# Attention scores from q and k as loaded: float32 matmuls on two row halves of the array in place of float32r parts

## Chip, core and metric

One core of a Trainium2 chip. The metric is the device time of one execution in microseconds (us); lower is better. A Trainium2 core has five engines with queues of their own: TensorE (PE in the rows, with its weight loads as PEld), VectorE (DVE), ScalarE (ACT), GpSimd (POOL) and SyncE (SP), which issues most of the DMAs.

## What is computed

Attention with a threshold, then a sum of four experts, then a squared-ReLU network. All inputs are float32, but for the last network's weights, which come as float64 and are narrowed on the chip during the experts. Batch 2, 8 heads, 576 positions, head size 64; 1152 tokens of 512 features.

```python
scores = q @ k.T / sqrt(64)                       # per head, 576 x 576
thresh = max(scores, axis=-1) - tau
p = exp(where(scores >= thresh, scores, -1e9) - max)
x = (p / (sum(p, axis=-1) + 1e-9)) @ v            # heads side by side: 1152 x 512
y = sum over e of pn[:, e] * (relu(x @ w1[e]) @ w2[e])   # 4 experts, 1024 wide
out = relu(y @ w_in) ** 2 @ w_out                 # 2048 wide
```

## The kernel before, in words

**Two stages.** Attention works through eight *units* u; a unit is a pair of heads z = 0, 1 of one batch entry. Behind it comes a dense stream: `first` and `second` for four experts and for the two halves of the last network, with weights split into a high and a low float32r part.

**A unit.** The 576 queries of a head are four tiles of 128 and a rest of 64; the rests of both heads share a ninth tile, the corner (k = 8). `qk` (L333) makes a score tile of 128 queries by 576 keys in PSUM, as two halves g of 288 keys. `rowmax` (L348) takes the negated maximum on VectorE; `threshold` (L352) makes one number per query from it and tau, as a difference of two 128x1 tensors; `expo` (L365) is the exponential on ScalarE; `mask` (L369) on VectorE compares the scores with the threshold, multiplies, and sums the row; `addeps` and `recip` give the row's reciprocal; `norm` (L385) multiplies p with it on GpSimd, and `norm_corner` (L393) does so for 64 more columns of the corner on VectorE. `turn` transposes p on TensorE (L402), `evac` copies the result to SBUF, mostly on ScalarE, and `pv` (L451) multiplies with v: float32 matmuls of 288 columns, the two heads on two halves of the array's columns. A mask frees the PSUM tile of its scores; there are three such tiles.

**q and k.** float32r matmuls take operands that are rounded, so `qk` works on parts. For units 1 to 7, `load_qk` (L263) loads 128 rows of 640 columns each of q and k, `q_scale` (L316) multiplies q by 1/8 on ScalarE, `high` (L307) rounds on ScalarE, `low` (L311) subtracts on GpSimd, and `stack` (L320) copies the parts between partitions by twelve DMAs a unit of 160 KB, so that a tile holds the high part of q over its low part, and two tiles hold the high and the low part of k twice. Two matmuls per half, one with each k tile, then give all four products; a score tile is four matmuls, the corner's eight. For unit 0, `start_qk` (L281) loads q and k of each head by a broadcast DMA that writes both halves of the partitions,

```python
nc.sync.dma_start(r[:, y], src[0][y * D:(y + 1) * D].unsqueeze(0).to_broadcast([2, D, r.shape[-1]]))   # L288
```

and makes the parts in place on three engines.

**Order.** The order on every engine is written out: each step of unit u is an event at the time u plus a number from the tables `WHEN` and `OWN`, and the events are sorted (L531). So TensorE meets scores, transposes and PV runs of neighbouring units in turn, and a step waits, in its place, for what it needs; what is behind it on its engine waits too.

Of the kernel before, what the change touches and what calls it, by code (L numbers as in the profile page):

```python
# [17 lines left out]
B, H, S, D = 2, 8, 576, 64  # L18
# [3 lines left out]
P = 128  # L22
NP = H // 2
NU = B * NP
QT = S // P
SQ = (QT + 1) * P
REM = S - QT * P
KC = 2 * QT + 1
# [31 lines left out]
    "q_scale": -2.100,  # L60
    "q_high": -1.890,
    "q_low": -1.695,
    "k_high": -1.456,
    "k_low": -1.025,
    "stack": (-0.339, -0.512, -1.282, -0.686),
    "load_v": 0.670,
# [45 lines left out]
        "q_scale": -12.152,  # L112
        "q_high": -9.978,
        "q_low": -9.096,
        "k_high": -12.288,
        "k_low": -10.414,
        "stack": (-9.241, -9.711, -7.013, -4.366),
    },
    2: {
        "load": -14.310,  # L120
        "q_scale": -7.271,
        "q_high": -4.013,
        "q_low": -1.805,
        "k_high": -10.466,
        "k_low": -6.537,
        "stack": (-1.315, -3.462, -1.279, -0.580),
    },
# [30 lines left out]
def attention_moe_kernel(ctx, tc, qT, kT, vp, tau, probs, wa, wb, wc, wd, out):  # L158
    nc = tc.nc
# [14 lines left out]
    qsc = const.tile([P, 1], F32, name="qsc")  # L174
    tneg = const.tile([P, 1], F32, name="tneg")
# [74 lines left out]
    pt_p = tail.enter_context(tc.tile_pool(name="pt", bufs=2))  # L250
# [22 lines left out]

    def new_qk(u):
        qs[u] = qk_p.tile([P, 2, SQ], F32R, tag="q1", name=f"q1{u}")
        ks[u] = (
            qk_p.tile([P, 2, SQ], F32R, tag="k1", name=f"k1{u}"),
            qk_p.tile([P, 2, SQ], F32R, tag="k2", name=f"k2{u}"),
        )

    def start_qk():  # L281
        new_qk(0)
        stage = pt_p.tile([P, KC, S], F32, tag="pt", name="stage").rearrange("p c s -> p (c s)")
        rq = stage[:, :2 * SQ].rearrange("p (y n) -> p y n", y=2)
        rk = stage[:, 2 * SQ:4 * SQ].rearrange("p (y n) -> p y n", y=2)
        for y in range(2):
            for r, src in ((rk, kT), (rq, qT)):
                nc.sync.dma_start(r[:, y], src[0][y * D:(y + 1) * D].unsqueeze(0).to_broadcast([2, D, r.shape[-1]]))  # L288
        q1, (k1, k2) = qs[0], ks[0]
        nc.vector.tensor_scalar(rq[:, 0], rq[:, 0], qsc, None, ALU.mult)  # L290
        nc.gpsimd.tensor_mul(rq[:, 1, P:], rq[:, 1, P:], qsc.to_broadcast([P, SQ - P]))
        nc.scalar.copy(k1[:, 0], rk[:, 0])
        nc.vector.tensor_sub(k2[:, 0], rk[:, 0], k1[:, 0].bitcast(F32))
        nc.scalar.copy(q1[:, 0, :P], rq[:, 0, :P])
        nc.vector.tensor_sub(q1[D:P, 0, :P], rq[D:P, 0, :P], q1[D:P, 0, :P].bitcast(F32))
        nc.scalar.copy(k1[:, 1], rk[:, 1])
        nc.vector.tensor_sub(k2[:, 1], rk[:, 1], k1[:, 1].bitcast(F32))
        nc.scalar.activation(q1[:, 1, :P], rq[:, 1, :P], AF.Copy, scale=qsc)
        nc.vector.scalar_tensor_tensor(  # L299
            q1[D:P, 1, :P], rq[D:P, 1, :P], qsc[D:P], q1[D:P, 1, :P].bitcast(F32), ALU.mult, ALU.subtract  # L300
        )
        nc.scalar.copy(q1[:, 0, P:], rq[:, 0, P:])
        nc.gpsimd.tensor_sub(q1[D:P, 0, P:], rq[D:P, 0, P:], q1[D:P, 0, P:].bitcast(F32))
        nc.scalar.copy(q1[:, 1, P:], rq[:, 1, P:])
        nc.gpsimd.tensor_sub(q1[D:P, 1, P:], rq[D:P, 1, P:], q1[D:P, 1, P:].bitcast(F32))

    def high(u, n):  # L307
        parts.setdefault(u, {})[n] = t = raw_p.tile([P, SQ], F32R, tag=f"high{n}", name=f"high{n}_{u}")
        nc.scalar.copy(t, raws[u][n])

    def low(u, n):  # L311
        raw, t = raws[u][n], parts[u][n].bitcast(F32)
        parts[u][2 + n] = o = raw_p.tile([P, SQ], F32R, tag=f"low{n}", name=f"low{n}_{u}")
        nc.gpsimd.tensor_sub(o, raw, t)

    def q_scale(u):  # L316
        rq = raws[u][0]
        nc.scalar.activation(rq, rq, AF.Copy, scale=qsc)

    def stack(u, n):  # L320
        if u not in qs:
            new_qk(u)
        for y in range(2):
            src = parts[u][n][y * D:(y + 1) * D].bitcast(F32)
            for z in ((n // 2,), (0, 1))[n % 2]:
                o = (qs[u], ks[u][n // 2])[n % 2]
                nc.sync.dma_start(o[z * D:(z + 1) * D, y].bitcast(F32), src)

    HW = S // 2
    W = 2 * QT + 1  # L330
    s_t, p_t, nm_t, th_t, sm_t, r_t, pt_t, t_t, pv_t, xs_t = ({} for _ in range(10))

    def qk(u, k):  # L333
        i, z = divmod(k, 2)
        s = ps_s.tile([P, 2, 512], F32, tag="s", name=f"s{u}_{k}")
        for g in range(2):
            a = g * HW
            if i < QT:
                ops = [(qs[u][:, z, i * P:(i + 1) * P], k[:, z, a:a + HW]) for k in ks[u]]
            else:  # L340
                ops = [
                    (qs[u][:, y, QT * P:], k[:, y, a + y * REM:a + y * REM + HW]) for y in range(2) for k in ks[u]
                ]
            for x, (w, k) in enumerate(ops):
                nc.tensor.matmul(s[:, g, :HW], w, k, start=(x == 0), stop=(x == len(ops) - 1))  # L345
        s_t[u, 2 * i + z] = s[:, :, :HW]

# [61 lines left out]
    idle = [0]  # L409
# [65 lines left out]
    def at(u, t, f, *args):  # L475
        events.append((u + t, len(events), f, (u,) + args))

    for u in range(NU):
        when = {**WHEN, **OWN.get(u, {})}
# [14 lines left out]
        if u:  # L494
            at(u, when["load"], load_qk)
            at(u, when["q_scale"], q_scale)
            for n, t in enumerate(when["stack"]):
                at(u, t, stack, n)
            for n, x in enumerate("qk"):
                at(u, when[x + "_high"], high, n)  # L500
                at(u, when[x + "_low"], low, n)

# [259 lines left out]
```

## Time and profile before

| | |
|---|---|
| median of 3 runs | 802.04 us (801.55 to 802.53) |
| the profiled execution | 802.34 us |
| its span, first to last instruction | 800.0 us |
| mean granted TensorE clock | 0.978 |
| busy in the span | PE 755.7, DVE 367.5, ACT 292.3, POOL 275.5 us |
| bytes moved by DMA | 75.66 MB |

The profile is of one execution. A group of rows gives a view of it: *slices* cut the span in 40 equal parts, each digit the busy tenths of one; *stretches* give the busy time of each engine between two times; a *timeline* lists instructions by their start, with repeats of one form taken together, and in brackets how long the engine had been idle and what released it; *groups* take together all instructions of a line and form. A DMA row gives the time that its issue took on the queue. Starts and durations of matmuls overlap, since they are pipelined, so the step from one start to the next says more than a duration. PV appears as two records per float32 matmul. Times count from the span's start.

### The profile page before, as it was taken

Reading aid. Unit: us, or ns where it says so; the run is one execution under the profiler, and the core shown is the slowest. Engines: PE = TensorE matmul, PEld = TensorE weight load, DVE = VectorE, ACT = ScalarE, POOL = GpSimd, SP = SyncE. Lnnn points to the kernel's source line nnn. Section 1 sums busy time; section 2 is a strip of 40 time slices with the busy share of each in tenths; the row PEclk is TensorE's granted clock in tenths of the full one; section 3 lists DMA queues with packets and bytes.
Section 4 is the critical chain, followed back from the end, with each engine's and each line's share of the span. In section 5 each row is a group of like instructions: output and inputs, shape, how many; then the busy total and the mean of one; then the engine's idle time right before and its main releaser. Section 6 shows DMA issues by size and latency. Waiting matters only on the chain.

```text
span 800.0 us, 10387 instructions
## 1 busy us (share of the span) xinstructions
PE 755.7 (94%) x4052; PEld 657.1 (82%) x4052; DVE 367.5 (46%) x723; ACT 292.3 (37%) x524; POOL 275.5 (34%) x201
## 2 busy tenths in 40 slices
PE   3289999999999999999999999999999999999998
PEld 2266666657898889988899888998889988899886
DVE  0499999993644336643354333664422210022111
ACT  1378888763342013321133201331225531255200
POOL 0387777761323112220222211221126641266300
PEclk7589999999999999999999999999999999999999
DMA  1477685300534314441344332333101110010011
GB/s 42 121 204 211 150 229 131 99 18 1 197 132 153 110 67 131 133 132 39 132 132 125 94 110 74 125 132 106 39 27 53 53 54 26 27 53 1 17 50 53
DMA packets 28056, 75.66 MB, mean 95 GB/s; under 512 B 3816, under 2 KB 3816, under 8 KB 28008
## 3 DMA queue, kind: packets, MB, share of 16 engines
q1 hardware_dynamic: 27976, 75.01, 30.4%
q8 instruction: 32, 0.52, 0.3%
q14 instruction: 16, 0.13, 0.1%
q0 software_dynamic: 32, 0.00, 0.0%
HBM read 50.48 MB, written 10.75 MB: 77 GB/s over the span
## 4 chain that ended last, share of the span: by engine, by line
PE 77%; DVE 12%; DMA 4%; issue 3%; ACT 2%; SPq 1%; ACTq 0%; POOL 0%; DVEq 0%; POOLq 0%
PE po L633 37%; PE ph L556 36%; DVE p L374 5%; DMA stage<-in_qT_dram 3%; DVE th L354 3%; DVE nm L350 2%; PE pv L451 2%; PE s L345 1%; SPq L288 1%; DMA wraw<-in_wa_dram 1%; PE t L402 1%; DVE pm L374 1%; ACT p L367 1%; DVE sm L379 1%; PE x2t L650 0%
## 5 line engine op out<-in xcount | busy, mean ns | idle before, releaser
L212 POOL TENSOR_TENSOR wlo<-wraw,whi 128x1024 fp32r<-128x1024 f32 x48 | 115.5, 2405 | 375.0 <-ACT whi L210 323.3
L556 PE MATMUL ph<-xhi,whi 128*128 128x384 f32 x576 | 196.1, 340 | 1.9 <-DVE hlo L600 1.8
L556 PE MATMUL ph<-xlo,whi 128*128 128x384 f32 x576 | 194.8, 338 | 0.0
L556 PE MATMUL ph<-xhi,wlo 128*128 128x384 f32 x576 | 194.8, 338 | 0.0
L633 PE MATMUL po<-whi,hhi 128*128 128x512 f32 x432 | 168.8, 391 | 0.0
L633 PE MATMUL po<-whi,hlo 128*128 128x512 f32 x432 | 168.2, 389 | 0.0
L633 PE MATMUL po<-wlo,hhi 128*128 128x512 f32 x432 | 168.1, 389 | 0.0
L556 PEld LDWEIGHTS ph<-xhi,whi 128*128 128x128 f32 x576 | 108.1, 188 | 4.3 <-issue 2.8
L556 PEld LDWEIGHTS ph<-xlo,whi 128*128 128x128 f32 x576 | 108.1, 188 | 0.2
L556 PEld LDWEIGHTS ph<-xhi,wlo 128*128 128x128 f32 x576 | 108.1, 188 | 0.0
L345 PE MATMUL s<-k,q 128*128 128x288 f32 x320 | 64.7, 332 | 34.2 <-DVE q L299 12.4
L633 PEld LDWEIGHTS po<-whi,hlo 128*128 128x128 f32 x432 | 81.1, 188 | 17.1
L633 PEld LDWEIGHTS po<-wlo,hhi 128*128 128x128 f32 x432 | 81.1, 188 | 16.4
L633 PEld LDWEIGHTS po<-whi,hhi 128*128 128x128 f32 x432 | 81.1, 188 | 16.3
L345 PEld LDWEIGHTS s<-k,q 128*128 128x128 f32 x320 | 48.2, 202 | 44.6 <-DVE q L299 12.8
L604 DVE SCALAR_TENSOR_TENSOR u<-ph,u 128x384 f32<-128x384 f32 x48 | 26.8, 558 | 123.5 <-ACT u L603 123.5
L600 DVE SCALAR_TENSOR_TENSOR hlo<-ph,hhi 128x384 fp32r<-128x384 f32 x96 | 53.0, 554 | 61.6 <-ACT hhi L599 61.5
L238 ACT ACTIVATE wide<-wide 128x512 f32<-128x512 f32 x32 | 21.4, 669 | 162.6 <-DVE dbl L237 159.4
L391 POOL TENSOR_TENSOR p<-p,r 128x576 f32<-128x576 f32 x60 | 68.0, 1148 | 31.6 <-DVE th L354 9.8
L599 ACT ACTIVATE hhi<-ph 128x384 fp32r<-128x384 f32 x96 | 45.7, 489 | 84.4 <-PE ph L556 84.4
L611 POOL TENSOR_TENSOR hlo<-u,hhi 128x384 fp32r<-128x384 f32 x48 | 48.5, 1016 | 32.7 <-ACT hhi L610 32.7
L640 DVE SCALAR_TENSOR_TENSOR acc<-po,pn,acc 128x512 f32<-128x512 f32 x27 | 20.3, 751 | 83.8 <-PE po L633 83.8
(83 smaller groups left out, 773.7 us busy)
## 6 DMA issues: line engine op xcount, KB each, us to landing
wraw<-in_wa_dram SPq DMA_DIRECT2D x16, 512.0 KB, 4.1
wide<-in_wc_dram SPq DMA_DIRECT2D x16, 512.0 KB, 3.7
wraw<-in_wb_dram SPq DMA_DIRECT2D x16, 512.0 KB, 4.3
narrow<-dbl SPq DMA_DIRECT2D x32, 256.0 KB, 2.4
wide<-in_wd_dram SPq DMA_DIRECT2D x16, 512.0 KB, 3.6
wraw<-narrow SPq DMA_DIRECT2D x16, 512.0 KB, 3.2
k<-high SPq DMA_DIRECT2D x28, 160.0 KB, 3.0
k<-low SPq DMA_DIRECT2D x28, 160.0 KB, 5.0
```

The costliest lines, as they stand in the source:

```text
L212: engine.tensor_sub(lo, t, hi.bitcast(F32))
L238: nc.scalar.activation(m, m, AF.Square)
L345: nc.tensor.matmul(s[:, g, :HW], w, k, start=(x == 0), stop=(x == len(ops) - 1))
L354: nc.vector.tensor_sub(th_t[u, k], tneg, nm_t[u, k])
L374: nc.vector.scalar_tensor_tensor(p, s_t.pop((u, k)), th_t[u, k], p, ALU.is_ge, ALU.mult, accum_out=sm_t[u, i][:, z:z + 1])
L391: nc.gpsimd.tensor_mul(p, p, r_t[u, i][:, z:z + 1].to_broadcast([P, S]))
L556: nc.tensor.matmul(o, w, m, start=a, stop=b)
L599: nc.scalar.activation(oh, p, AF.Relu)
L600: nc.vector.scalar_tensor_tensor(ol, p, 0.0, oh.bitcast(F32), ALU.max, ALU.subtract)
L604: nc.vector.scalar_tensor_tensor(r, p, 0.0, r, ALU.max, ALU.mult)
L611: nc.gpsimd.tensor_sub(ol, r, oh.bitcast(F32))
L633: nc.tensor.matmul(o, w, m, start=(x == 0), stop=(x == len(ops) - 1))
```

## The change

The scores become true float32 matmuls on q and k as they were loaded. The host lays q out as 64 rows for both heads, and repeats it in the other 64 partitions; k is laid out so that partitions 0 to 63 hold its first 288 keys and partitions 64 to 127 the other 288 (head 0, head 1 with its rest first, and head 1 in plain order, which the corner uses). Half g of a score tile is then one matmul over rows 64g to 64g + 63 of the array, and a tile is two matmuls, which write separate parts of the score tile; the corner's are four, each on 64 rows and 64 columns. The parts, their copies, `start_qk`'s work on three engines and their events go. A unit loads 576 KB of q and 432 KB of k, into four buffers instead of two; unit 0 loads them head by head. Two more edits: `threshold` becomes a scalar operation (nm times -1, plus tneg read as one number per partition), and `norm_corner` moves to GpSimd, except at the end, where the kernel puts normalisation on VectorE. The other entries of the tables stay.

```diff
     def load_qk(u):
-        rq = raw_p.tile([P, SQ], F32, tag="rq", name=f"rq{u}")
-        rk = raw_p.tile([P, SQ], F32, tag="rk", name=f"rk{u}")
-        nc.sync.dma_start(rq, qT[u])
-        nc.sync.dma_start(rk, kT[u])
+        qs[u] = qk_p.tile([P, 2, S], F32, tag="q", name=f"q{u}")
+        ks[u] = qk_p.tile([P, 3, HW], F32, tag="k", name=f"k{u}")
+        if u:
+            nc.sync.dma_start(qs[u], qT[u])
+            nc.sync.dma_start(ks[u], kT[u])
+        else:
+            for z in range(2):
+                nc.sync.dma_start(qs[u][:, z], qT[u][:, z])
+                nc.sync.dma_start(ks[u][:, z:z * 2 + 1], kT[u][:, z:z * 2 + 1])
...
+    def q_scale(u):
+        nc.scalar.activation(qs[u], qs[u], AF.Copy, scale=qsc)
...
     def start_qk():
-        new_qk(0)
...
+        load_qk(0)
+        for z in range(2):
+            nc.vector.tensor_scalar(qs[0][:, z], qs[0][:, z], qsc, None, ALU.mult)
...
     def qk(u, k):
...
+        cols = slice(i * P, min(i * P + P, S))
+        for y in (z,) if i < QT else range(2):
+            o = s if i < QT else s[y * REM:(y + 1) * REM]
+            for g in range(2):
+                rows = slice(g * D, (g + 1) * D)
+                nc.tensor.matmul(
+                    o[:, g, :HW], qs[u][rows, y, cols], ks[u][rows, y if i < QT else 2 * y], start=True, stop=True
+                )
...
     def threshold(u, k):
-        nc.vector.tensor_sub(th_t[u, k], tneg, nm_t[u, k])
+        nc.vector.tensor_scalar(th_t[u, k], nm_t[u, k], -1.0, tneg, ALU.mult, ALU.add)
...
     def norm_corner(u):
-        nc.vector.tensor_scalar(p[:, S:], p[:, QT * P:S], r_t[u, QT], None, ALU.mult)
+        if idle[0]:
+            nc.vector.tensor_scalar(p[:, S:], p[:, QT * P:S], r_t[u, QT], None, ALU.mult)
+        else:
+            nc.gpsimd.tensor_mul(p[:, S:], p[:, QT * P:S], r_t[u, QT].to_broadcast([P, REM]))
```

Removed with no successor: `new_qk`, `high`, `low`, `stack`, the pool `raw`, and the table entries `q_high`, `q_low`, `k_high`, `k_low` and `stack`.

What the engines then meet, in order, at three places (the numbers in a name count tiles as they are made, and differ between the kernels). **SP's queue from the start**, before, with the copies of unit 1 at its end:

```order
L288 DMA stage<-in_kT_dram 128x1x640
L288 DMA stage<-in_qT_dram 128x1x640
L288 DMA stage<-in_kT_dram 128x1x640
L288 DMA stage<-in_qT_dram 128x1x640
L530 DMA pr<-in_probs_dram 128x36
L266 DMA rq_171<-in_qT_dram 128x640
L267 DMA rk_172<-in_kT_dram 128x640
L266 DMA rq_198<-in_qT_dram 128x640
L267 DMA rk_199<-in_kT_dram 128x640
L327 DMA k_236<-high_1_215 64x640 x4
```

and after the change:

```order
L257 DMA q_115<-in_qT_dram 128x576
L258 DMA k_116<-in_kT_dram 128x288
L257 DMA q_115<-in_qT_dram 128x576
L258 DMA k_116<-in_kT_dram 128x576
L468 DMA pr<-in_probs_dram 128x36
L253 DMA q_152<-in_qT_dram 128x1152
L254 DMA k_153<-in_kT_dram 128x864
L253 DMA q_175<-in_qT_dram 128x1152
L254 DMA k_176<-in_kT_dram 128x864
```

The four broadcasts have become four plain loads, and nothing is copied between partitions behind the loads. **TensorE late in a steady unit** (t a transpose run, s a score run, pv a PV run), before:

```order
L402 MATMUL t_0_1052<-ident,p_0_886 128x128 x4
L345 MATMUL s_7_1057<-k_600,q_599 128x288
L345 MATMUL s_7_1057<-k_601,q_599 128x288
L345 MATMUL s_7_1057<-k_600,q_599 128x288
L345 MATMUL s_7_1057<-k_601,q_599 128x288
L451 MATMUL pv_0_1043<-pt_801,rv_815 64x288 x2
L402 MATMUL t_7_1074<-ident,p_3_808 128x128 x4
```

and after the change, with the corner behind it:

```order
L345 MATMUL t_0_1094<-ident,p_0_953 128x128 x4
L283 MATMUL s_7_1099<-k_564,q_563 128x288 x2
L394 MATMUL pv_0_1087<-pt_877,rv_890 64x288 x2
L345 MATMUL t_7_1114<-ident,p_3_1108 128x128 x4
L283 MATMUL s_8_1123<-k_564,q_563 64x288 x4
```

The runs stand in the same turn; a score run has two matmuls instead of four, the corner's four instead of eight. **VectorE around a corner**, before:

```order
L379 TENSOR_SCALAR sm_3_1095<-sm_3_1095 128x2
L354 TENSOR_TENSOR th_0_1161<-tneg,nm_0_1138 128x1
L379 TENSOR_SCALAR sm_4_1153<-sm_4_1153 128x1
L383 RECIPROCAL r_3_1172<-sm_3_1095 128x2
L354 TENSOR_TENSOR th_1_1174<-tneg,nm_1_1155 128x1
L383 RECIPROCAL r_4_1177<-sm_4_1153 128x1
L395 TENSOR_SCALAR pm_1126<-pm_1126,r_4_1177 128x64
```

and after the change:

```order
L319 TENSOR_SCALAR sm_3_900<-sm_3_900 128x2
L294 TENSOR_SCALAR th_0_957<-nm_0_936,tneg 128x1
L319 TENSOR_SCALAR sm_4_949<-sm_4_949 128x1
L323 RECIPROCAL r_3_966<-sm_3_900 128x2
L294 TENSOR_SCALAR th_1_968<-nm_1_951,tneg 128x1
L323 RECIPROCAL r_4_971<-sm_4_949 128x1
L314 SCALAR_TENSOR_TENSOR p_0_953,sm_0_984<-s_0_907,th_0_957,p_0_953 128x576
```

The thresholds are another operation in the same place, and the corner's product is gone from this engine; the next mask follows at once.

## Rows read from the trace of the kernel before

**Rows 1.** The page's slices of the span: TensorE's busy tenths, 20 us a slice.

```profile
PE   3289999999999999999999999999999999999998
```

**Rows 2.** Stretches: length, engines' busy us (instructions), granted clock, DMA share, GB/s.

```profile
0.00:20.00 20.00, 6.50 (x28) 5.96 (x28) 1.89 (x5) 2.51 (x4) 1.41 (x7) 0.77 0.11 42
20.00:31.25 11.25, 0.21 (x1) 0.00 (x0) 0.83 (x1) 0.72 (x1) 0.00 (x0) 0.50 0.49 149
...
122.27:140.95 18.68, 17.48 (x123) 12.06 (x121) 18.58 (x49) 15.02 (x30) 14.67 (x14) 1.00 0.49 125
```

**Rows 3.** Timeline of VectorE at the start: start, duration, instruction [idle before, releaser].

```profile
7.51 0.15 DVE L523 TENSOR_SCALAR qsc<-tau_t 128x1 f32<-128x1 f32 x1 [7.51 <-DMA tau_t<-in_tau_dram]
...
17.22 0.55 DVE L290 TENSOR_SCALAR stage<-stage,qsc 128x640 f32<-128x640 f32 x1 [9.33 <-DMA stage<-in_qT_dram]
...
32.59 0.76 DVE L350 TENSOR_REDUCE nm<-s 128x1 f32<-128x576 f32 x1
```

**Rows 4.** Timeline of SP's queue, its first load: start and time to issue.

```profile
0.75 0.70 SPq L288 DMA_DIRECT2D stage<-in_kT_dram  x1
```

**Rows 5.** Timelines of GpSimd and VectorE around 116 us.

```profile
115.29 2.25 POOL L391 TENSOR_TENSOR p<-p,r 128x576 f32<-128x576 f32 x2 [1.18 <-DVE r L383]
...
116.42 1.13 DVE L354 TENSOR_TENSOR th<-tneg,nm 128x1 f32<-128x1 f32 x1
```

**Rows 6.** Groups of VectorE, four units: line, form, count, busy, mean ns, idle before.

```profile
L354 DVE TENSOR_TENSOR th<-tneg,nm 128x1 f32<-128x1 f32 x36 | 18.3, 509 | 0.1
L395 DVE TENSOR_SCALAR pm<-pm,r 128x64 f32<-128x64 f32 x4 | 4.5, 1117 | 0.1
...
L379 DVE TENSOR_SCALAR sm<-sm 128x2 f32<-128x2 f32 x16 | 2.9, 181 | 0.0
...
L379 DVE TENSOR_SCALAR sm<-sm 128x1 f32<-128x1 f32 x4 | 0.6, 140 | 0.0
```

**Rows 7.** Waits of TensorE, four units: us in total, times, longest.

```profile
PE s L345 <- DVE p L374: 3.7, 7, 1.0
```

**Rows 8.** Timelines of VectorE (first and last unit) and TensorE (last unit).

```profile
36.86 0.96 DVE L354 TENSOR_TENSOR th<-tneg,nm 128x1 f32<-128x1 f32 x1
...
168.63 2.41 DVE L354 TENSOR_TENSOR th<-tneg,nm 128x1 f32<-128x1 f32 x2
...
172.03 0.79 PE L345 MATMUL s<-k,q 128*128 128x288 f32 x4 [1.48 <-DVE p L374]
```

**Rows 9.** DMA issues of the span: count, KB each, median us to landing.

```profile
rv<-in_vp_dram SPq DMA_DIRECT2D x8, 320.0 KB, 5.3
...
rq<-in_qT_dram SPq DMA_DIRECT2D x7, 320.0 KB, 12.1
```

**Rows 10.** Groups of the whole span, ScalarE's scaling of q.

```profile
L318 ACT ACTIVATE rq<-rq,qsc 128x640 f32<-128x640 f32 x7 | 5.9, 836 | 0.0
```

**Rows 11.** Timeline of TensorE in steady units: start, first start to last end.

```profile
115.56 0.77 PE L345 MATMUL s<-k,q 128*128 128x288 f32 x4
116.26 0.71 PE L451 MATMUL pv<-pt,rv 128*64 128x288 f32 x4
116.90 0.66 PE L402 MATMUL t<-ident,p 128*128 128x128 f32 x4
117.31 1.31 PE L345 MATMUL s<-k,q 128*128 128x288 f32 x8
118.46 0.60 PE L402 MATMUL t<-ident,p 128*128 128x128 f32 x4
...
121.50 1.19 PE L451 MATMUL pv<-pt,rv 128*64 128x288 f32 x8
122.62 0.66 PE L402 MATMUL t<-ident,p 128*128 128x128 f32 x4
...
129.75 0.78 PE L345 MATMUL s<-k,q 128*128 128x288 f32 x4
130.36 0.60 PE L429 MATMUL tr<-ident,p 128*128 128x128 f32 x4
```

More of the change, by code (lines that the diff above doesn't have):

```diff
@@ L60 @@
     "q_scale": -2.100,
[L61 to L65, printed above, removed]
     "load_v": 0.670,
@@ L112 @@
         "q_scale": -12.152,
[L113 to L117, printed above, removed]
     },
@@ L121 @@
         "q_scale": -7.271,
[L122 to L126, printed above, removed]
     },
@@ L254, in attention_moe_kernel @@
     head = ExitStack()
-    raw_p = head.enter_context(tc.tile_pool(name="raw", bufs=2))
-    qk_p = head.enter_context(tc.tile_pool(name="qk", bufs=2))
+    qk_p = head.enter_context(tc.tile_pool(name="qk", bufs=4))
     p_p = head.enter_context(tc.tile_pool(name="p", bufs=6))
@@ L259, in attention_moe_kernel @@
     ps_s = head.enter_context(tc.tile_pool(name="ps_s", bufs=3, space=PSUM))
-    raws, parts, qs, ks, vs = {}, {}, {}, {}, {}
+    qs, ks, vs = {}, {}, {}
+    HW = S // 2
     def load_qk(u):
-        rq = raw_p.tile([P, SQ], F32, tag="rq", name=f"rq{u}")
-        rk = raw_p.tile([P, SQ], F32, tag="rk", name=f"rk{u}")
-        nc.sync.dma_start(rq, qT[u])
-        nc.sync.dma_start(rk, kT[u])
-        raws[u] = (rq, rk)
+        qs[u] = qk_p.tile([P, 2, S], F32, tag="q", name=f"q{u}")
[7 more added lines that the diff above has]
+                nc.sync.dma_start(ks[u][:, z:z * 2 + 1], kT[u][:, z:z * 2 + 1])
     def load_v(u):
@@ L272, in load_v @@
         nc.sync.dma_start(vs[u], vp[u])
[L274 to L279, printed above, removed]
-    def start_qk():
-        new_qk(0)
[L283 to L327, printed above, removed]
@@ L329, in attention_moe_kernel @@
-    HW = S // 2
+    def q_scale(u):
+        nc.scalar.activation(qs[u], qs[u], AF.Copy, scale=qsc)
+    def start_qk():
+        load_qk(0)
+        for z in range(2):
+            nc.vector.tensor_scalar(qs[0][:, z], qs[0][:, z], qsc, None, ALU.mult)
     W = 2 * QT + 1
@@ L335, in qk @@
         s = ps_s.tile([P, 2, 512], F32, tag="s", name=f"s{u}_{k}")
[L336 to L345, printed above, removed]
+        cols = slice(i * P, min(i * P + P, S))
[6 more added lines that the diff above has]
+                )
         s_t[u, 2 * i + z] = s[:, :, :HW]
@@ L496, in attention_moe_kernel @@
             at(u, when["q_scale"], q_scale)
[L497 to L501, printed above, removed]
     def load_weights(u):
@@ L719, in pairs_t @@
         return a.reshape(NU, 2, S, D).transpose(0, 1, 3, 2)
-    qp = _np.zeros((NU, 2, D, SQ), q.dtype)
-    qp[..., :m] = pairs_t(q)[..., :m]
-    for z in range(2):
-        qp[:, z, :, m + z * REM:m + (z + 1) * REM] = pairs_t(q)[:, z, :, m:]
-    kt = pairs_t(k).copy()
-    kt[:, 1] = _np.concatenate([kt[:, 1, :, m:], kt[:, 1, :, :m]], axis=-1)
+    qp = pairs_t(q).transpose(0, 2, 1, 3)
+    kt = pairs_t(k)
+    rolled = _np.concatenate([kt[:, 1, :, m:], kt[:, 1, :, :m]], axis=-1)
+    kt = _np.stack([kt[:, 0], rolled, kt[:, 1]], axis=2).reshape(NU, D, 3, 2, S // 2).transpose(0, 3, 1, 2, 4)
     vh = v.reshape(NU, 2, S, D)
@@ L738 @@
     given = {
-        "qT": qp.reshape(NU, P, SQ),
-        "kT": _np.concatenate([kt, kt[..., :REM]], axis=-1).reshape(NU, P, SQ),
+        "qT": _np.concatenate([qp, qp], axis=1),
+        "kT": kt.reshape(NU, P, 3, S // 2),
         "vp": vp,
```

## The prediction

> **What bounds the kernel now.** I read the slices of the span first. From 200 us on TensorE's tenths stand at 9 in every slice but the last [rows 1]: the experts are one dense stream of matmuls, whose weights are loaded and split by events placed relative to it. A microsecond saved before them is a microsecond saved at the end, and nothing in the change touches them. So the attention stage is the whole question, and it has three stretches.
>
> *The start.* Over the first 20 us the DMA share is 0.11 at 42 GB/s and the granted clock averages 0.77 [rows 2]. VectorE has its scale factor at 7.51 us but gets q only at 17.22, and the first row maximum starts at 32.59 [rows 3]. Four broadcast loads stand at the head of SP's queue, the first issued at 0.75 [rows 4].
>
> *The steady units* (one pair of heads each). In the unit from 122.27 to 140.95 VectorE is busy for 18.58 of 18.68 us, TensorE for 17.48 [rows 2]. VectorE is not working all that time: a threshold of one element per partition starts at 116.42 and lasts 1.13 us, ending when GpSimd's pair of normalisations, started at 115.29 for 2.25 us, ends [rows 5]. Over four units thresholds average 509 ns, and the 64-column corner normalisation 1117 ns, while a 128x1 scalar operation takes 140 ns [rows 6]. So the bound reads VectorE, held by GpSimd, with TensorE about 1 us behind. What TensorE waits for in four units is 3.7 us behind the mask [rows 7], 0.92 us a unit, out of 18.68 - 17.48 = 1.2 us idle.
>
> *The end of attention.* Two thresholds take 2.41 us at 168.63, and TensorE idles 1.48 us before its next scores, behind the mask [rows 8].
>
> **The change, part by part.** *The start.* The broadcasts, their high and low parts and the copies go; four plain loads of 128 partitions and two scalings on VectorE stay. Plain loads of 320 KB land 5.3 us after issue (v) or 12.1 us after it (q, in the median; the first of them stood behind the broadcasts) [rows 9]. Issued 0.7 us apart from 0.75 on [rows 4], the third load, q of the second head, which VectorE scales before it takes any maximum, lands at 2.15 + 5.3 = 7.5 us, or at 14.3 by the far end. I take the first, since the broadcasts ahead are gone. tau arrives at 7.51 [rows 3]. Then qsc and tneg (0.4 us), two scalings (0.55 us for 640 columns [rows 3], so at most 1.1 us) and what is left of the first score's own time behind the second scaling (I allow 0.3 us): the first maximum starts at about 9.3 us in place of 32.59, so **-23.3 us**; -24.2 if tau, no longer behind broadcasts, comes before that load (7.5 + 0.55 + 0.3 = 8.4), and -17.3 by the late end. The second unit's loads now follow at once; its scaling on ScalarE has two exponentials ahead of it.
>
> *Thresholds and corner on VectorE.* The threshold becomes a scalar operation with one tensor input. Nearest is the 128x1 addition of epsilon: 140 ns, against 181 for the 128x2 form [rows 6]. Per unit this removes 9 x (0.509 - 0.140) = 3.3 us, and the corner's move removes 1.1, so VectorE needs 18.58 - 4.4 = 14.2 us. GpSimd gains a 128x64 product (between the 0.14 us of VectorE's smallest row and 1.1 us, half of GpSimd's two products of 576 columns [rows 5, 6]) and loses the two 640-column subtractions; it has idle time in every unit and I cost this at nothing. ScalarE loses two casts; its scaling grows from 640 to 1152 columns, 836 ns [rows 10] to at most 1.8 x 836 = 1.5 us: also nothing, since the scaling comes two units ahead of its use. If either cover went, the normalised p for the transposes would be late next. On SP, twelve copies between partitions a unit go and two larger loads replace two small ones; with buffers for four units no load is waited for.
>
> *TensorE.* This is what then binds. Today a four-matmul score run takes 0.61 us when a transpose follows (129.75 to 130.36), 0.70 when PV follows (115.56 to 116.26); the corner's eight take 1.15 (117.31 to 118.46) [rows 11]. No float32 score matmul on half of the rows exists in this trace; the nearest rows are PV, float32 matmuls of the same 288 columns on two halves of the array's columns. Four PV records, that is two matmuls, take 0.64 us to the next transpose (116.26 to 116.90); eight take 1.12 (121.50 to 122.62) [rows 11]. So one pair costs 0.48 us, a run of it 0.16 us more behind it, and 0.70 - 0.61 = 0.09 ahead. A float32 score pair, priced alike, costs 0.73 us: +0.12 a run, up to +0.20 for weights of 128 columns rather than 64 and the slower first transpose. Eight runs at the middle, +0.16: +1.28; the corner, four matmuls on four quarters, 1.15 to 0.73: -0.42. TensorE's unit goes from 17.48 to **18.34 us**. Both ends: if a change between row halves and the full array cost nothing, a run, the corner's too, would cost the 0.61 of today's, so 17.48 - 0.54 = 16.9; if it cost twice PV's 0.25, 0.98 a run, 9 x 0.98 - (8 x 0.61 + 1.15) = +2.8, so 20.3. I take PV's, the only mode change with rows.
>
> The Trainium skill, "TensorEngine Tiling (Array Packing)", section Tiling Modes, says that changing the tiling mode, not merely the tile, drains the engine; it speaks against this change, since the scores now change mode before and behind every run. By it the sum is the one with 18.34; without drains it would be the one with 16.9.
>
> The 0.92 us a unit behind the mask goes, since the mask comes earlier; the other 0.28 stays. The unit becomes 18.34 + 0.28 = 18.6 instead of 18.68: TensorE takes VectorE's place as the bound, with **-0.1 a unit, -0.5 us over seven units**. What vanishes on VectorE is thus mostly not gained.
>
> *First unit and end.* The first unit has almost no transposes and stays with VectorE: the threshold at 36.86 alone held it for 0.96 us [rows 8]; with the smaller holds around it I take **-1.3 us** (0 if GpSimd's other work holds it as long; -2 at most). The end's 1.48 us [rows 8] goes: **-1.5 us**.
>
> **Sum**, against the profiled execution's 802.34 us (span 800.0 and 2.3 around it; 0.3 over the median of 802.04): 802.34 - 23.3 - 0.5 - 1.3 - 1.5 = 775.7; I say **776 us**.
>
> **The rivals.**
> *The halves do not overlap (slower).* If the second half's matmul starts only when the first has ended, a run costs 0.96 + 0.25 = 1.21 us: +0.60 for eight runs, +0.06 for the corner: +4.9 a unit, 22.4 + 0.3 = 22.7 us on TensorE. Seven units add 28 us, more than the 26 won elsewhere: 776 + 28 = 804 us. It decides from about 3.8 us more a unit, that is 0.4 us a run. For it: rows of half-array matmuls by rows are missing. Against: PV's column halves overlap, for eight records of 288 columns fit into 1.12 us, and the two score halves are written to separate parts of the score tile, 512 columns apart. Chance 0.08.
> *The threshold is still held.* Then the change does not do what it says on VectorE: it saves only the corner there (17.5 us a unit), the first unit and the end keep their holds, and the time is 776 + 2.8 = 779 us. For it: the 128x2 scalar form is slower, 181 against 140 ns [rows 6]; against: the form here is 128x1. Chance 0.07. The Trainium skill, "SBUF — State Buffer", Who interferes with whom, says scalar operations can enter two-port modes and then contend with GpSimd; by it the rival would hold if one element per partition qualified.
> *A late start.* Loads at the far end of 12.1 us, or unit 0 at the low clock, which is 0.50 in the stretch before the scores today [rows 2]: up to 6 us later, 780 us. Chance 0.10.
> *Cheap mode changes.* TensorE's unit at 16.9 + 0.28 = 17.2, -1.5 us in each of seven units in place of -0.1: 776 - 10 = 766 us. For it: nothing here shows a row drain. Chance 0.15.
>
> **How the numbers follow.** My case has 0.60. The range takes in the cheap and the late start and most of the dearer mode change: from 766 less 0.9 for an early tau and 0.7 for the first unit's -2, 764, to 776 + 6 (start) + 7 (a unit at 19.6), 789 us. The non-overlapping halves stay outside. A measurement here can tell 0.2%, 1.6 us, from no change. Only that rival lies above 802, and its 804 straddles the band: slower 0.07, same 0.03, faster 0.90.
>
> **What would show it.** Right: the first maximum at 8 to 11 us; thresholds near 0.15 us with GpSimd busy; two score matmuls starting nearly together; a unit of 18 to 19 us in which TensorE is busy throughout and VectorE has gaps; the last transposes some 26 us earlier. Wrong: score runs of 1.2 us or more, units over 20 us, thresholds that end with GpSimd's rows, or a first maximum after 14 us.

## The result, and the profile after

The changed kernel takes **771.23 us** (median of 4 runs, 769.99 to 771.41) against 801.79 of the kernel before beside it: a ratio of 0.9614 (0.9598 to 0.9631), 30.6 us less. 776 was forecast, in a range of 764 to 789. The profiled execution took 769.99 us, with a span of 768.2. Ratios, here and below, leave out one execution in a slower state (824.83 us, of the kernel with both matmuls on the same rows).

The page's slices of the span, TensorE's busy tenths, now 19.2 us a slice, which answer to [rows 1]:

```profile
PE   6999999999999999999999999999999999999997
```

The gaps at the head are gone but for the first slice. VectorE's timeline at the start answers to [rows 3]:

```profile
6.95 0.15 DVE L461 TENSOR_SCALAR qsc<-tau_t 128x1 f32<-128x1 f32 x1 [6.95 <-DMA tau_t<-in_tau_dram]
...
7.27 0.95 DVE L270 TENSOR_SCALAR q<-q,qsc 128x576 f32<-128x576 f32 x2
8.64 0.76 DVE L290 TENSOR_REDUCE nm<-s 128x1 f32<-128x576 f32 x1 [0.43 <-PE s L283]
```

The first maximum starts at 8.64 in place of 32.59. Both scalings of q follow at once when tau has landed: tau, not q, is what the start waits for.

For the units I cut the span at the masks of the corners, one for each unit. First comes the sum of the seven stretches between these masks before (columns as in [rows 2], after "sum" the length); then, after the change, the start, a stretch at the lower clock, two of the units, and the sum of all seven.

```profile
sum 128.95, PE 120.78 PEld 82.83 DVE 126.56 ACT 103.37 POOL 97.29; mean PE 17.25 PEld 11.83 DVE 18.08 ACT 14.77 POOL 13.90
```
```profile
0.00:8.64 8.64, 5.96 (x30) 5.59 (x32) 1.19 (x4) 1.49 (x2) 1.40 (x7) 1.00 0.68 196
13.00:23.20 10.20, 8.87 (x36) 3.88 (x33) 9.62 (x31) 5.97 (x9) 6.36 (x6) 0.50 0.33 117
...
24.19:40.43 16.24, 15.43 (x103) 7.97 (x102) 14.95 (x46) 13.45 (x24) 10.36 (x10) 1.00 0.19 65
...
112.02:129.90 17.88, 17.76 (x123) 9.27 (x121) 16.41 (x47) 13.25 (x27) 11.87 (x13) 1.00 0.07 20
...
sum 123.64, PE 122.15 PEld 63.02 DVE 109.12 ACT 97.69 POOL 81.33; mean PE 17.45 PEld 9.00 DVE 15.59 ACT 13.96 POOL 11.62
```

A late unit takes 17.88 us instead of 18.68 [rows 2], and TensorE is busy for 17.76 of it: TensorE is the bound. VectorE's groups over four of these units answer to [rows 6]:

```profile
L294 DVE TENSOR_SCALAR th<-nm,tneg 128x1 f32<-128x1 f32 x36 | 7.4, 206 | 0.1
L319 DVE TENSOR_SCALAR sm<-sm 128x2 f32<-128x2 f32 x16 | 6.5, 409 | 0.0
...
L319 DVE TENSOR_SCALAR sm<-sm 128x1 f32<-128x1 f32 x4 | 0.6, 144 | 0.0
```

A threshold takes 206 ns instead of 509; the addition of epsilon, 128x2, takes 409 instead of 181, so part of the hold has moved there. What VectorE waits for most in these units is now TensorE's scores (us in total, times, longest):

```profile
DVE nm L290 <- PE s L283: 3.9, 13, 0.8
```

TensorE's timeline in a unit answers to [rows 11], with the corner last:

```profile
93.62 0.66 PE L345 MATMUL t<-ident,p 128*128 128x128 f32 x4
94.21 0.76 PE L283 MATMUL s<-k,q 64*128 64x288 f32 x4
94.90 0.46 PE L394 MATMUL pv<-pt,rv 128*64 128x288 f32 x2
...
126.67 0.71 PE L283 MATMUL s<-k,q 64*64 64x288 f32 x8
127.50 0.63 PE L345 MATMUL t<-ident,p 128*128 128x128 f32 x4
```

A float32 matmul is two records here, as with PV. A score pair takes 0.69 us to the next run, the corner 0.83 in place of 1.15. Four transposes take 0.59 us to the pair behind them, where the four ahead of the corner in [rows 11] took 0.41.

### The profile page after: what moved, and what is told of

It reads as the page before. It is cut to its first block, busy times and chain, and to the rows that moved or that the text cites. A ratio compares the mean times of both kernels' runs of the same rounds, so it can differ in the third digit from the quotient of the medians.

```text
span 768.2 us, 10174 instructions
## 1 busy us (share of the span) xinstructions
PE 754.8 (98%) x4052; PEld 632.1 (82%) x4052; DVE 343.1 (45%) x712; ACT 282.7 (37%) x504; POOL 252.6 (33%) x192
## 4 chain that ended last, share of the span: by engine, by line
PE 94%; DVE 2%; issue 1%; POOL 1%; DMA 1%; ACT 1%; DVEq 0%; POOLq 0%; ACTq 0%
PE ph L494 39%; PE po L571 38%; PE pv L394 6%; PE s L283 5%; PE t L345 4%; DVE p L314 1%; DMA tau_t<-in_tau_dram 1%; POOL p L331 1%; PE x2t L588 1%; PE tr L372 1%; DVE nm L290 0%; ACT p L307 0%; PE tc L379 0%; DVE th L294 0%; POOL pm L331 0%
## 5 line engine op out<-in xcount | busy, mean ns | idle before, releaser
L571 PEld LDWEIGHTS po<-whi,hhi 128*128 128x128 f32 x432 | 81.1, 188 | 16.4
L283 PE MATMUL s<-k,q 64*128 64x288 f32 (+1 forms) x320 | 56.3, 471 | 5.0 <-DVE th L294 3.6
L290 DVE TENSOR_REDUCE nm<-s 128x1 f32<-128x576 f32 x72 | 54.0, 752 | 12.0 <-PE s L283 11.8
```

The lines of the kernel that those rows point to most:

```text
L283: nc.tensor.matmul(o[:, g, :HW], qs[u][rows, y, cols], ks[u][rows, y if i < QT else 2 * y], start=True, stop=True)
L290: nc.vector.tensor_reduce(nm_t[u, k], s_t[u, k], AX.XY, ALU.max, negate=True)
L571: nc.tensor.matmul(o, w, m, start=(x == 0), stop=(x == len(ops) - 1))
```

## The experiments

**The parts one by one.** Three kernels put pieces of the change into the kernel before. The first only replaces the start's four broadcast loads:

```diff
-                nc.sync.dma_start(r[:, y], src[0][y * D:(y + 1) * D].unsqueeze(0).to_broadcast([2, D, r.shape[-1]]))
+                for h in range(2):
+                    nc.sync.dma_start(r[h * D:(h + 1) * D, y], src[0][y * D:(y + 1) * D])
```

> The kernel before, and only the four loads of the start are changed: each broadcast load of two copies becomes two plain loads of 64 partitions. The new scores, threshold and corner are not in it. Theory S, as in the prediction: the start is limited by the broadcast form of the loads. The splits stay on the path, so the first maximum falls from 32.6 us to about 11 (9 to 14), and the time is about 780 us (778 to 784). Rival: the splitting of q and k, not the loads, holds the start; then the first maximum stays above 25 us and the time above 794 us.

780.61 us, ratio 0.9737 (0.9723 to 0.9752), as theory S has it. VectorE's timeline at the start of this kernel:

```profile
4.88 0.15 DVE L524 TENSOR_SCALAR qsc<-tau_t 128x1 f32<-128x1 f32 x1 [4.88 <-DMA tau_t<-in_tau_dram]
...
6.16 0.55 DVE L291 TENSOR_SCALAR stage<-stage,qsc 128x640 f32<-128x640 f32 x1 [0.88 <-DMA stage<-in_qT_dram]
...
10.31 0.76 DVE L351 TENSOR_REDUCE nm<-s 128x1 f32<-128x576 f32 x1
```

22.3 of the 23.95 us at the start come from the form of four loads. With the splits (the making of high and low parts) still there, the first maximum is only 1.67 us later than in the changed kernel.

The second has only the two edits on VectorE, the `threshold` and `norm_corner` lines of the change's diff.

> The kernel before with the new threshold and the corner's scaling on GpSimd, nothing else. It takes VectorE's 18.58 us a unit off the path without touching TensorE's work. Theory A, busy time is work (as the prediction took it): TensorE's 17.48 us plus 0.28 idle is left, the unit falls from 18.68 to about 17.76, and the time by 7 to 9 us, to about 794. Theory B, part of the 17.48 is hidden waiting for VectorE, since the modelled ends of matmuls run into the next start: the unit falls to 16.5 to 17.1, and the time by 13 to 17 us, to 785 to 789. Rival C: GpSimd's added corner (its own queue of splits stays) holds something instead, and the time is within 2 us of before.

793.34 us, 0.9895 (0.988 to 0.991), 8.7 us less. Two of its seven stretches and their sum, and below them two of VectorE's groups in its unit from 119.60 and the one after:

```profile
101.46:119.60 18.14, 16.62 (x118) 11.48 (x117) 16.38 (x48) 15.57 (x29) 15.01 (x14) 1.00 0.95 253
...
137.02:153.90 16.88, 16.85 (x123) 12.00 (x122) 16.23 (x47) 13.30 (x27) 13.40 (x14) 1.00 0.48 122
...
sum 120.99, PE 116.92 PEld 82.03 DVE 111.62 ACT 101.96 POOL 98.24; mean PE 16.70 PEld 11.72 DVE 15.95 ACT 14.57 POOL 14.03
```
```profile
L354 DVE TENSOR_SCALAR th<-nm,tneg 128x1 f32<-128x1 f32 x18 | 3.7, 205 | 0.1
L379 DVE TENSOR_SCALAR sm<-sm 128x2 f32<-128x2 f32 x8 | 3.3, 417 | 0.0
```

The time fits theory A, but the mechanism is B's. The same 123 matmul records that stood at 17.48 us busy in the unit before now stand at 16.85, with nothing taken from TensorE. So 0.63 us of the 17.48 was waiting, hidden under ends that are modelled. The steps from start to start show where. First two rows of the kernel before, in its unit of [rows 2], then two of this kernel:

```profile
124.98 0.66 PE L402 MATMUL t<-ident,p 128*128 128x128 f32 x4
126.64 0.79 PE L345 MATMUL s<-k,q 128*128 128x288 f32 x4 [1.00 <-DVE p L374]
```
```profile
140.81 0.66 PE L405 MATMUL t<-ident,p 128*128 128x128 f32 x4
141.22 0.77 PE L345 MATMUL s<-k,q 128*128 128x288 f32 x4
```

The step from the transposes to the scores is 1.66 us before and 0.41 here, so that 1.25 us were waited, of which the profile counts 1.00 as idle. In that unit of the kernel before three of the nine such steps are long, 1.70 us together over the 0.41 of the rest, with 1.20 us of the unit counted idle; here none is long.

The total stays near A's because the seven units gain unevenly, 0.49, 0.66, 1.52, 0.34, 1.26, 1.79 and 1.90 us in turn: B's unit is reached only late. The one shown first has TensorE busy for 16.62 of 18.14 us at a DMA share of 0.95. What holds that one I did not settle.

The third has both, so all of the change but the new scores.

> The kernel before with both: plain loads at the start, the new threshold and the corner's scaling on GpSimd. The scores stay the old ones of split q and k. It has all of the change but the new scores. If the new scores cost TensorE 0.16 us a run as worked out (1.3 us a unit, some 9 to 10 us in all) and TensorE is the bound, this kernel is faster than the changed one: 802 less 21 for the start less 15 for the units, 763 to 768 us, against 771. If the new scores are not dearer than the old, or the splits' transfers and GpSimd work hold the units, it takes 771 us or more.

771.65 us, 0.9626 (0.961 to 0.9642): the same as the changed kernel within the intervals. The two parts add up (21.45 + 8.72 = 30.2 us, measured 30.4), and the new scores add nothing measurable to them. I had expected 763 to 768; the gain of the units was the part I had put too high. The profile shows what balances. One unit of it, and the sum of seven:

```profile
113.93:130.79 16.86, 16.82 (x123) 12.00 (x122) 16.21 (x48) 13.29 (x27) 13.40 (x14) 1.00 0.48 122
...
sum 119.71, PE 116.76 PEld 82.05 DVE 110.01 ACT 101.94 POOL 98.14; mean PE 16.68 PEld 11.72 DVE 15.72 ACT 14.56 POOL 14.02
```

Against it the changed kernel loses 3.93 us in seven units (123.64 - 119.71; in a late one 17.88 - 16.86 = 1.02). It wins the same back earlier: its first corner's mask is at 24.19 us, and here at 28.02, at the end of a stretch that here still holds the splits of units 0 and 1.

**Do the halves overlap?** Both matmuls of a pair on the same rows:

```diff
-                rows = slice(g * D, (g + 1) * D)
+                rows = slice(0, D)
```

> The changed kernel with both matmuls of a score pair on rows 0 to 63. It leaves out the scores of the second half of the keys (those of the first half stand in their place), so that its output isn't the reference's; the number and the shape of the instructions are the same. Theory: the two float32 matmuls of a pair run beside one another only because they stand on different halves of the rows. On the same rows they run one after the other, at 288 columns and about 0.48 us more a run, 9 runs a unit, 4.3 us a unit: the unit goes from 17.9 to about 22.2 and the time to about 803 us (795 to 808). Rival: they do not overlap as work, or the second is hidden elsewhere; then the time stays within 3 us of 771.

This kernel leaves out the scores of the other half of the keys. It took 818.4 us in the median of four (811.9 to 824.83), ratio 1.0179 (1.0126 to 1.0232). TensorE's timeline, and two stretches:

```profile
149.24 1.23 PE L283 MATMUL s<-k,q 64*128 64x288 f32 x4
150.41 1.19 PE L394 MATMUL pv<-pt,rv 128*64 128x288 f32 x8
```
```profile
8.00:52.00 44.00, 43.29 (x110) 25.65 (x111) 25.99 (x74) 19.36 (x30) 14.43 (x14) 0.50 0.27 103
148.80:170.82 22.02, 22.02 (x122) 12.50 (x122) 15.76 (x47) 13.46 (x26) 11.86 (x13) 1.00 0.05 16
```

A run takes 1.17 us instead of 0.69: the 0.48 expected, and 4.14 us a unit. So the pair does overlap, and for that it needs the two row halves. The time went past the range expected because of the clock: the granted clock stayed at 0.50 (1.2 GHz) from 8 to 52 us, though TensorE was busy for 43.29 of these 44 us; in the changed kernel it is at 0.50 only in 13.0 to 23.2. The unit from 31.82 us takes 29.09, the later ones 21.2 to 22.7, and the executions of 811.9, 815.5 and 821.29 us had mean granted clocks of 0.978, 0.973 and 0.964.

**Does VectorE still matter?** The changed kernel with the old `threshold` and `norm_corner`:

```diff
-        nc.vector.tensor_scalar(th_t[u, k], nm_t[u, k], -1.0, tneg, ALU.mult, ALU.add)
+        nc.vector.tensor_sub(th_t[u, k], tneg, nm_t[u, k])
...
```

> The changed kernel with the old threshold (a tensor subtraction) and the corner's scaling back on VectorE; new scores and new loads stay. Theory: TensorE, at 17.8 us a unit, and VectorE with its old edits, at up to 18.6, nearly tie, so that the unit returns to 18.2 to 18.7 and the time rises by 3 to 7 us to 774 to 778. Rival: with the splits gone from GpSimd, which are part of what the threshold was held by, VectorE gets below TensorE even with the old edits, and the time stays within 1.5 us of 771.

772.3 us, 0.9625 (0.9609 to 0.9641), below the 774 to 778 expected. One unit, and the threshold's group over 75 to 150 us:

```profile
113.53:131.74 18.21, 18.09 (x125) 9.41 (x123) 18.11 (x48) 13.18 (x26) 11.67 (x12) 1.00 0.06 19
```
```profile
L294 DVE TENSOR_TENSOR th<-tneg,nm 128x1 f32<-128x1 f32 x37 | 17.6, 481 | 0.2
```

The old form is still held (481 ns) without the splits, and VectorE is full again; the seven units take 2.9 us more (126.49 against 123.64). In the medians 1.1 us are left, inside the intervals, so the size stays open. In the kernel before the same edits were worth 8.7 us: with the new scores TensorE is so close behind that little of it is left.

Four of these kernels, all with plain loads at the start, now stand side by side:

| | old forms on VectorE | new forms |
|---|---|---|
| old scores | 780.61 us | 771.65 us |
| new scores | 772.3 us | 771.23 us |

Either part gives nearly the whole gain behind the loads, and the other then adds at most 1.1 us.

**Can the price of a run be halved?** Two table times of units 2 to 6 put runs 3 and 4, and 6 and 7, together:

```diff
-    "qk": (-0.291, -0.119, 0.007, 0.173, 0.244, 0.384, 0.504, 0.574, 0.694),
+    "qk": (-0.291, -0.119, 0.007, 0.243, 0.244, 0.384, 0.573, 0.574, 0.694),
```

> The changed kernel with two times of the table moved for the units 2 to 6, so that the score runs 3 and 4, and 6 and 7, stand next to one another on TensorE. No instruction is added or taken away. Theory: the new scores cost TensorE time at the borders between them and the other products; two runs side by side have one pair of borders instead of two, which saves 0.2 to 0.3 us a pair, 0.4 to 0.6 us a unit, 2 to 3 us in all: 768 to 769. Rival: the later run makes its maximum and exponential late, VectorE or TensorE waits, and the time is 771 or more.

772.07 us, 0.9623 (0.9608 to 0.9637): a miss. In a late unit only the pair 6 and 7 came to stand together, and that unit, shown here, is 0.19 us longer than 17.88 while TensorE is busy 0.07 us less:

```profile
95.20:113.27 18.07, 17.69 (x123) 9.35 (x121) 15.99 (x47) 14.21 (x28) 11.89 (x13) 1.00 0.07 19
```

The pair itself takes 1.18 us to the next run (106.95 to 108.13) instead of twice 0.69, but the later run comes late for VectorE, which waits 1.6 us for scores in this unit and 0.7 in the same one of the changed kernel. What a saved border is worth to the whole is not settled by this.

**tau, and the clock.** In the changed kernel GpSimd issues tau's load at 1.43 us. Here SP's queue loads it first:

```diff
-    nc.gpsimd.dma_start(tau_t, tau.to_broadcast([P, 1]))
+    nc.sync.dma_start(tau_t, tau.to_broadcast([P, 1]))
```

> The changed kernel with the threshold tau loaded by SP's queue, ahead of q and k, instead of by GpSimd's. In the changed kernel the load is issued at 1.43 us and the scaling of q starts at 6.95, when it has landed, while q and k lands earlier. Theory: tau is what the start waits for now; it lands about 2 us earlier, the first maximum moves from 8.6 to 6.5 or 7, and the time falls by 1.5 to 2.5 us, to 769 to 770. Rival: q and k, each pushed 0.45 us later behind it, or the halved clock that follows, take it back; then within 0.8 us of 771.

769.21 us, 0.9589 (0.9575 to 0.9604). tau arrives at 3.86 and the first maximum starts at 7.46, since now q and then the first scores are waited for:

```profile
3.86 0.15 DVE L461 TENSOR_SCALAR qsc<-tau_t 128x1 f32<-128x1 f32 x1 [3.86 <-DMA tau_t<-in_tau_dram]
...
6.05 0.52 DVE L270 TENSOR_SCALAR q<-q,qsc 128x576 f32<-128x576 f32 x1 [0.74 <-DMA q<-in_qT_dram]
7.46 0.76 DVE L290 TENSOR_REDUCE nm<-s 128x1 f32<-128x576 f32 x1 [0.88 <-PE s L283]
```

To this kernel the next adds work for TensorE in unit 0; `fill` makes n transpositions of the identity:

```diff
+    for k, n in ((2, 8), (3, 4), (4, 4), (5, 3)):
+        at(0, OWN[0]["qk"][k] + 1e-4, fill, n)
```

> The changed kernel with tau by SP's queue, and with 19 more 128x128 transpositions of the identity on TensorE, set in the gaps behind the third to sixth score run of unit 0. They compute nothing that is used. In the kernel with tau by SP, TensorE is idle in 8.0 to 10.0 us and in shorter gaps to 13, and its granted clock is 0.5 from 13.7 to 23. Theory K: the low clock holds unit 0; with the gaps filled the clock stays at 1.0, unit 0 ends 1.5 to 3 us earlier, and the time is 766 to 768. Rival V: in unit 0 VectorE is busy 14.62 of 15.64 us, so that the clock is hidden whatever it does; the clock rises or not, and the time stays within 0.8 us of 769.2.

770.99 us, 0.9615 (0.9602 to 0.9628): no gain, and 1.8 us above 769.21, where V allowed 0.8. First unit 0 of the kernel with tau by SP, from its first maximum to its corner, then of the one with filling, and three stretches inside that:

```profile
7.46:23.10 15.64, 11.28 (x52) 5.43 (x48) 14.62 (x43) 9.59 (x13) 6.76 (x6) 0.69 0.59 227
```
```profile
7.77:24.69 16.92, 13.14 (x71) 7.61 (x71) 14.71 (x44) 9.59 (x13) 6.75 (x6) 0.83 0.58 219
```
```profile
8.80:11.02 2.22, 2.22 (x8) 1.24 (x8) 0.85 (x2) 0.55 (x2) 0.00 (x0) 0.50 1.02 414
11.02:12.55 1.53, 1.53 (x11) 1.36 (x9) 1.53 (x5) 1.53 (x2) 0.00 (x0) 0.65 1.03 421
12.55:22.00 9.45, 6.70 (x45) 3.41 (x45) 9.41 (x30) 6.03 (x9) 4.51 (x5) 1.00 0.28 111
```

From 12.55 to 22.00 us the clock was at 1.0 (2.4 GHz), where it is 0.50 from 13.7 on without the filling, and VectorE is busy for 9.41 of these 9.45 us. The corner came 1.59 us later. That delay stands ahead of the first filling, at 11.02: the second head's q is scaled at 7.34 us instead of 6.05, and the second maximum starts at 10.17 instead of 8.38. From there to the corner it is 14.52 us, against 14.72 without filling. So unit 0 is VectorE's, as rival V says, and by these two profiles the low clock costs it no more than some 0.2 us.

**A better version.** The new scores are cheap at the start and dear later, so three kernels give the first units the new scores and the others the old ones, with the edits on VectorE and tau by SP. The first does so for unit 0 alone:

```diff
     def qk(u, k):
...
+        if u:
...
+                    ops = [(qs[u][:, z, i * P:(i + 1) * P], k[:, z, a:a + HW]) for k in ks[u]]
...
+        else:
...
+                        o[:, g, :HW], qs[u][rows, y, cols], ks[u][rows, y if i < QT else 2 * y], start=True, stop=True
```

> Unit 0 with the new scores, from q and k as loaded, without splits; units 1 to 7 with the old scores of split q and k; new threshold, corner on GpSimd, tau by SP's queue. It takes from each version the part that measured better: the start of the changed kernel (first maximum at 8.64 us, corner of unit 0 at 24.2) and the units of the kernel with old scores (119.7 us from the first corner to the last, against 123.6). Expected by adding: 771.2 less 3.9 for the units, up to 2 more for tau, plus 0.8 for a longer end: 766 to 768. Rival: the splits and the loads of unit 1, in the start's shadow no longer, delay unit 1, and the time is 769 to 773.

770.04 us, 0.9599 (0.9585 to 0.9614): the rival's range, but unit 0 is late and not unit 1. Its unit 0:

```profile
8.18:28.09 19.91, 15.18 (x53) 8.37 (x54) 16.81 (x43) 10.70 (x16) 10.92 (x9) 0.51 0.84 232
```

It takes 19.91 us instead of the 15.64 of the kernel with tau by SP. Of these 4.3 us, 2.1 come before the second maximum (11.22 instead of 8.38 us, the first being at 8.18 and 7.46). Here q and k of unit 0 are twelve narrow loads, which SP issues until 8.8 us instead of 3.0, and TensorE waits 2.0 us for k. The rest lies behind, beside 4.2 us more of GpSimd's work, the splits of unit 1, and 2.2 us more on VectorE, where two 128x2 additions take 1.35 and 1.06 us. The next kernel takes out the splits, but not the narrow loads; it gives two units the new scores:

```diff
-        if u:
+        if u > 1:
             for g in range(2):
...
     2: {
-        "load": -14.310,
+        "load": -4.0,
```

> Units 0 and 1 with the new scores, from q and k as loaded; units 2 to 7 with the old scores of split q and k, and the splits of unit 2 moved from the middle of unit 0 to its end; new threshold, corner on GpSimd, tau by SP's queue. In the hybrid before it, unit 1's splits ran beside unit 0, and unit 0's corner came at 28.1 us instead of 23.1 to 24.2. Theory: with them gone unit 0 takes what it takes in the changed kernel (corner at 23 to 24.5), and the units from 2 on take what they take with the old scores (17.5, 17.6, 17.4, 16.9, 17.0 against 18.3, 18.1, 17.9, 17.9, 17.9), so that the time is 769.2 less 3 to 4: 765 to 767. Rival: what was saved in unit 0 is lost in unit 2, whose splits now fall into a stretch where the engines are full; 768 to 771.

788.36 us, 0.9828 (0.9813 to 0.9842): a miss. Unit 0 still takes 20.41 us, so the splits were not what held it alone. Most of the loss is a fault of mine, which SP's timeline shows:

```profile
17.61 0.43 SPq L267 DMA_DIRECT2D rk<-in_kT_dram  x1
37.31 0.33 SPq L266 DMA_DIRECT2D rq<-in_qT_dram  x1
...
38.18 2.74 SPq L335 DMA_DIRECT2D k<-high  x4
40.96 1.10 SPq L272 DMA_DIRECT2D rv<-in_vp_dram  x1
```

Unit 1's q stood in one of the two buffers for loads, where it was still read at 48.75 us. So the load of unit 3 waited at the head of SP's queue for the other, from 18 us until GpSimd had made unit 2's last low part at 37.3, and unit 2's copies and v of unit 0 waited behind it; TensorE then waited 8.4 us for that v. The last version takes that out, and loads q and k of units 0 and 1 in five loads each:

```diff
+            t = [wraw_p.tile([P, 2, 512], F32, tag="wraw", name=f"qk{u}_{n}").rearrange("p y n -> p (y n)") for n in range(3)]
...
+        "load_v": -12.0,
```

> As the kernel with two units of new scores, but with what jammed SP's queue there taken out: q and k of units 0 and 1 come in the changed kernel's layout in five loads a unit, unit 1's stand in the buffers of the expert weights, which are free until then, so that no later load waits for them, and unit 0's v is loaded ahead of unit 2's stacking. Units 2 to 7 keep the old scores. Theory: unit 0's corner at 23 to 24.5 us, unit 1 at about 16.5, units 2 to 7 at 16.9 to 17.6 instead of 17.9 to 18.3; the time is 769.2 less 3 to 4: 765 to 767. Rival: unit 2's splits, 1.6 us of ScalarE's casts and some 4 to 5 us of GpSimd, lie between unit 0 and unit 2 in a stretch where VectorE and TensorE are both full, and unit 1 or 2 is longer by what the others save; 768 to 771.

The changed kernel ran beside it:

> The changed kernel, unchanged, on the same chip as the run beside it, so that the two compare directly. Every theory expects 771, between 770 and 772.

**766.01 us**, 0.9553 (0.954 to 0.9567). The changed kernel took 770.61, 0.9609 (0.9596 to 0.9622), so this one is 4.6 us faster than it. Part of that is tau by SP, which alone stood at 0.9589 (0.9575 to 0.9604). Two of its stretches and the sum:

```profile
21.96:39.97 18.01, 15.41 (x103) 8.27 (x104) 17.19 (x46) 16.07 (x29) 14.68 (x13) 1.00 0.70 180
...
109.80:126.67 16.87, 16.84 (x123) 11.99 (x122) 16.23 (x48) 13.30 (x27) 13.41 (x14) 1.00 0.48 123
...
sum 121.66, PE 117.47 PEld 79.66 DVE 112.14 ACT 103.47 POOL 99.69; mean PE 16.78 PEld 11.38 DVE 16.02 ACT 14.78 POOL 14.24
```

A late unit takes 16.87 us. In the profiles this kernel's span is 4.0 us shorter than that of the kernel with tau by SP: 1.05 before the first maximum (6.41 us), 0.1 in unit 0, whose corner is at 21.96, 2.2 in the seven stretches and 0.7 behind them. Unit 1, beside which the splits of unit 2 now run, takes 18.01 us against 16.45, which I put down to them: the rival's part in it.

## Why the prediction was right, and where it was off

The profiled span is 31.8 us shorter: 23.95 before the first maximum, 1.39 between it and the first corner (16.94 to 15.55), 5.31 in the seven units, and 1.10 behind the last corner.

- **The start: right.** -23.3 forecast. The kernel with plain loads alone shows that the broadcasts were the cause. I had q land last, at 7.5 us; it was tau, at 6.95. The early bound, -24.2, is nearer by luck: it stood for a start that waits for q. Of its terms, the arrival came 0.55 us earlier, the scale factors and scalings took 0.23 less, and the first score 0.13 more. (The late-start rival, 6 us on 776, comes to 782 and not 780.)
- **The first unit: right by luck.** -1.3 forecast, from the hold of the thresholds. With the new threshold and the old scores unit 0 takes 17.38 us, no less than before; with the old threshold and the new scores it takes 15.42, and its thresholds average 163 ns. So it was not the threshold's new form that gave the 1.39 us, but what the new scores brought, most likely that no splits run beside it.
- **The end: right in kind.** -1.5 forecast. The hold lies in the last of the seven units, which went from 18.86 to 17.93 us and stays at 18.86 with the old forms on VectorE. The 1.10 us behind the last corner have no term in the forecast, and no run shows a cause: in two executions of the changed kernel that stretch took 620.37 and 620.83 us, and over all these kernels 620.08 to 622.20.
- **VectorE freed: right in kind.** 14.2 us a unit was forecast and 16.0 to 16.4 measured: 206 ns a threshold, not 140, and the 128x2 additions at 409. It changed nothing, since VectorE no longer binds. The rival "the threshold is still held" is out: 206 ns against 481 for the old form beside nearly the same GpSimd work. The rule of the Trainium skill, "SBUF — State Buffer", Who interferes with whom, that scalar operations can contend with GpSimd, is seen here at two elements per partition (409 ns), not at one (206).
- **The price of the new scores: right.** +0.86 us a unit forecast; 17.76 - 16.85 = +0.91 measured, with the same count of records. The 0.16 a run lies ahead of it, not behind: the transposes take 0.18 us more to the scores, and the step from scores to PV is 0.69 against 0.70. The corner gave 0.32, not 0.42. The rival of cheap mode changes is out, and so is the one without overlap. "TensorEngine Tiling (Array Packing)", Tiling Modes, in the Trainium skill says that a change of tiling mode drains the engine; the trace agrees in that the step into the pairs costs more (0.59 us against 0.41).
- **The step that failed: "TensorE's unit goes from 17.48 to 18.34 us" and "the other 0.28 stays".** The base was mis-sized. 17.48 was busy time with 0.63 us of hidden waiting in it; the work was 16.85. So the new unit is 17.76 and not 18.34, and 0.12 us of idle time is left, not 0.28: 17.88 against 18.6, below the 18 to 19 that was to show the forecast right. The seven units and the end together gave -5.31 in place of -0.5 - 1.5 = -2.0. Of the 5.75 us between the sum, 775.74, and the profiled 769.99, that is 3.31; the start gives 0.65, the first unit 0.09, the stretch behind the last corner 1.10, and the time around the span 0.60 (2.38 to 1.78).
- **The sentence "What vanishes on VectorE is thus mostly not gained"** holds for the changed kernel, for a reason that the forecast did not draw out: the new scores themselves spend it. With the old scores a late unit is 1 us shorter still.

## What to carry to other kernels

Where an engine with modelled ends waits in short pieces, its busy time is no measure of its work: count the same records in a stretch where nothing is waited for, or bound the work from below by steps from start to start. A change with several parts should be priced part by part, also against a version that leaves out the part it is named after: here the four loads gave 21.5 of the 30.6 us, and either the new scores or two small edits on VectorE gave nearly all of the rest. And a step that pays at the start, where splits and copies are on the path, may cost in the steady state: it can be used for the first units alone.

## What was not expected of the hardware

- A tensor subtraction of one element per partition took 481 to 509 ns on average beside GpSimd's normalisations; the same result by a scalar operation took 205 to 206. The 128x2 addition, whose code did not change, went from 181 to 409 and 417 ns when the threshold before it was no longer held.
- tau, 4 bytes a partition, landed at 6.95 us beside the changed kernel's loads (DMA share 0.68 up to 8.64 us), at 4.88 beside the smaller plain loads, and at 3.86 at the head of SP's queue.
- With both matmuls of a pair on the same rows, TensorE's granted clock stayed at 0.50 (1.2 GHz) for 44 us in which TensorE was busy for 43.29 us: up to 23.9 us with score matmuls of 64 rows alone, then with these, runs of four to eight transposes between them, and one PV run. In the filled kernel it was at 0.50 while only score matmuls ran (8.80 to 11.02), and at 1.0 (2.4 GHz) behind eight transposes of the identity that ran from 11.02 to 12.55.
